# Last attention blocks routed ahead of the early rows' first layer, and the early rows' second layer moved behind the barrier

## The chip, the cores and the metric

The kernel runs on one core of one Trainium2 chip. The metric is device time in microseconds (us) of one execution. Each number of the profile comes from one profiled execution of the kernel, in microseconds from the start of its span.

## The reference, cut to what matters

Chunked attention feeds a mixture of experts in which each token goes to one of eight experts.

```python
batch, n_heads, seq, head_dim = (4, 8, 768, 64); n_mem = 8
chunk, left_ctx, right_ctx = (32, 16, 8)
for c in range(seq // chunk):              # every chunk of 32 queries sees its neighbours and the memory
    scores = scale * q_c @ k_full.T
    out[:, :, c_start:c_end] = softmax(scores) @ v_full
x = out.transpose(0, 2, 1, 3).reshape(3072, 512)
logits = x @ w_gate                        # [3072, 8]
expert_idx = argmax(logits); gate_w = softmax(logits)[expert_idx]
for e in range(8):                         # rows of expert e, w1 [512, 1024], w2 [1024, 512], all float32
    y[rows of e] = relu(x[rows of e] @ w1[e]) @ w2[e]
return gate_w[:, None] * y
```

## The kernel before, in words

The 3,072 tokens are 32 blocks of 96. The loop in `ordinary` (`for i in range(NB)`) makes block i's scores, the values of block i-1 (`values`), and turns block i-2 for its logits (`turn_xb`). Blocks are routed in eight groups, the last two of which are blocks 26 to 28 and 29 to 31. Routing a group (`routed`) is a list of small steps: the best expert of each token, a one-hot matrix, two small matmuls that count how many earlier tokens went to the same expert (`rank`), then `own`, `row` and `where`, which give each token its row in `x_dram`. Only then a block may be scattered there: one indirect DMA on GpSimd per block (`scatter_one`, L848), made to wait for the TensorE instruction that was written down last before it (`behind`).

When 22 blocks are scattered, the first 256 rows of expert 0 are read back (`early_load`, `early_gather`). These are the early rows. Their expert is computed in `early_ops`: a transpose on VectorE (`turn_early`), eight pieces `first(f)` of the first layer (four matmuls of 256 columns each, then a relu on ScalarE, L1093), and before the barrier 384 of the 512 columns of the second layer for their first 128 rows (`part_of`, tile `py0`).

After the loop the code is written out by hand: it sets the order on every engine, since nothing reorders it. It interleaves the last values, the last three blocks' logits (`last_logits`, tile `lg`), the two last groups' routing, the early pieces, the six last scatters, and `count_up`. That counts the tokens of each expert (L973), works out the arm of code for each (`cases`), the first rows (`bases`, L999 to L1001), a check that all softmax sums are sound (`check_sums`, L901 to L903, then a matmul with `okn` and `most`, L1009, which gives `good`), and the row numbers (`rows`, L1025). The second weight matrix of expert 1 (2 MB, L1045) is loaded into the buffer in which the turned blocks (`xTs`) lay, so it waits for the last logits. `end_rows(0)` writes zeros behind expert 0's rows (L965) and needs `bases`.

Then comes a barrier: the sync engine (SP) waits for every DMA and engine (L1846), and every engine waits for the others, before the experts begin. Behind the barrier, `interlude(0)` loads expert 0's other rows (L1420, tile `xs`), opens `sum_r` with two small matmuls, and runs what is left of the early rows' second layer on TensorE (`sum_z`): the last 128 columns for the first 128 rows, then 512 columns for the second 128 rows. After it the first product of expert 0 (`sum_p`) starts. A matmul of float32 is two instructions here: a `first(f)` is eight in the trace, a second layer of 128 rows sixteen.

Of the kernel before, what the change touches and what calls it, by code (L numbers as in the profile page):

```python
# [22 lines left out]
QB = 96  # L23
# [48 lines left out]
NER = 256  # L72
# [10 lines left out]
PAGE = 256  # L83
EARLY_COLUMNS = 384
LB = 16
# [442 lines left out]
def ordinary(ctx, tc, q, k, v, mem_k, mem_v, moe_w_gate, moe_w1, moe_w2, out, good):  # L528
# [180 lines left out]
    def values(i, g, bank):  # L709
        s = st[i]  # L710
        if g == 0:
            s["x"] = xr[:, i % NXR, LB:DX]
        o = bank[0:QB, 0 : 4 * (D + 1)].rearrange("p (h d) -> p h d", h=4)
        for j in range(4):
            h = 4 * g + j
            mm(o[:, j], lhsT=s["ex"][:, h], rhs=s["v"][:, h, 0 : D + 1], start=True, stop=True)

        inv = inv_all[:, i, 4 * g : 4 * g + 4]
        nc.vector.reciprocal(inv, o[:, :, D])
        x = s["x"].rearrange("p (h d) -> p h d", h=H)  # L720
        nc.vector.tensor_tensor(x[:, 4 * g : 4 * g + 4], o[:, :, 0:D], bc(inv, 2, D), op=OP.mult)
    def turn_xb(i):
# [244 lines left out]

    def count_up():

        cnt = cur["bank"][:, 4 * (D + 1) + 8 * E : 4 * (D + 1) + 9 * E + 1]  # L970
        mm(cnt[:, 0:E], lhsT=ones[0:QB], rhs=seen[:, NB], start=True, stop=True)
        mm(cnt[:, E : E + 1], lhsT=ones[0:QB], rhs=okn, start=True, stop=True)
        nc.vector.tensor_tensor(count, cnt[:, 0:E], ebase, op=OP.subtract)  # L973
        nc.vector.tensor_tensor(count[:, 0:1], count[:, 0:1], n0, op=OP.subtract)
# [33 lines left out]
        nc.vector.tensor_scalar(most[:, 0:1], most[:, 0:1], float(XC), None, op0=OP.is_le)  # L1008
        nc.vector.tensor_scalar(most[:, 1:2], cnt[:, E : E + 1], float(QB * 2 * NB * H), None, op0=OP.is_equal)  # L1009
        nc.vector.tensor_tensor(most[:, 0:1], most[:, 0:1], most[:, 2:3], op=OP.mult)  # L1010
# [40 lines left out]

    early_ops = []

# [3 lines left out]

    def second_layer(py, g, fs, sl=slice(0, DM)):
        made = []
        for f in fs:  # L1060
            made.append(
                mm(
                    py,
                    lhsT=h0[:, f, 128 * g : 128 * g + 128],
                    rhs=ms[0]["w2"][:, f, sl],
                    start=f == 0,
                    stop=f == F // 128 - 1,
                )
            )
        return made[0], made[-1]  # L1070

    def early_out(g, py, sl=slice(0, DM)):
        return nc.scalar.activation(early["y", g][:, sl], py, AF.Copy, scale=lab0[:, g, 1:2])

    def early_rows():
# [6 lines left out]

        def first(f):
            ph = ps_s.tile([128, 2, 512], F32, tag="s", name="ph0")[:, 0, 0:NER]
            for c in range(DM // 128):
                mm(
                    ph,
                    lhsT=ms[0]["w1"][:, c, 128 * f : 128 * f + 128],
                    rhs=x0T[:, c],
                    start=c == 0,  # L1090
                    stop=c == DM // 128 - 1,
                )
            nc.scalar.activation(h0[:, f], ph, AF.Relu)  # L1093

        hold = {}

        def part_of(fs, sl):
            if fs[0] == 0:
                hold["y"] = ps_s.tile([128, 2, 512], F32, tag="s", name="py0")
            py = hold["y"][:, 0, 0 : sl.stop - sl.start]  # L1100
            second_layer(py, 0, fs, sl)
            if fs[-1] == F // 128 - 1:
                early_out(0, py, sl)

        early_ops.append(turn_early)
        for f in range(F // 128):
            early_ops.append(lambda f=f: first(f))
# [8 lines left out]
    with tc.manual_schedule():  # L1116
# [19 lines left out]
        for i in range(NB):  # L1136
# [11 lines left out]
            if i <= 23:  # L1148
                routing(1, "p")
            if i >= 1:  # L1150
                values(i - 1, 0, banks[0])
            need(i - 2, turn_xb)
# [3 lines left out]
            if i >= 1:  # L1156
                values(i - 1, 1, banks[1])
            if late:
                place_logits(*late)
            if i > 23:  # L1160
                routing(1, "p")
# [24 lines left out]

        do_early(1)
        n = NB

        def bank_pair():  # L1190
            banks = [ps_o.tile([128, 512], F32, tag="o", name="o") for _ in range(2)]
            cur["bank"] = banks[0]
            return banks
# [11 lines left out]
        routing(99, "v")  # L1205
# [5 lines left out]
        nc.vector.tensor_copy(*late)  # L1211
        do_early(1)
# [6 lines left out]
        banks = bank_pair()  # L1219
        late = last_logits(n - 1, banks[1])  # L1220
        nc.vector.tensor_copy(*late)
        fetch_piece(1)
        work.extend(routed(len(GROUPS) - 1))
        routing(99)
        check_sums()
        do_early(2)
        scatter_some(1)
        routing(1, "p")
        routing(99, "v")
        hold_back()  # L1230
        do_early(1)
        scatter_some(1)
        count_up()
# [5 lines left out]
        while spread:  # L1239
            scatter_some(1)  # L1240
            if len(early_ops) == 2:
                load_index(0)
            do_early(1)
        zeroed = end_rows(0)
# [403 lines left out]
    def interlude(e):  # L1648

        before = ("before", e)  # L1650
        if e == 0:
# [8 lines left out]
            for i in range(3):  # L1660
                sums1[0][0][i]()
            rest_of = slice(EARLY_COLUMNS, DM)
            last = Z[:, 1, 0 : DM - EARLY_COLUMNS]
            op("PE", lambda n: second_layer(last, 0, range(F // 128), rest_of), [], ["z1"], where=before)
            op("ACT", one_op(lambda: early_out(0, last, rest_of)), [], ["z1", "y00"])
            for part in range(4):
# [264 lines left out]
```

## Time and profile before

| | us |
|---|---|
| median of 3 runs (lowest, highest) | 489.65 (489.1, 490.19) |
| the profiled execution | 489.89 |
| its span, first to last instruction | 488.1 |
| attention, routing and early rows | 0 to 164 |
| barrier: TensorE from its last to its next matmul | 164 to 167.3 |
| rest of the early rows' second layer | 167.3 to 179 |
| eight experts | 179 to 480 |

The page counts how long each engine was busy. In 40 slices it also shows the clock that TensorE was granted. A row of the timeline has the start, the time, the engine (PE is TensorE's matmuls, PEld its weight loads, DVE VectorE, ACT ScalarE, POOL GpSimd, SP the sync engine; a q marks an instruction of the engine's queue), the line, the operation, what it writes and reads, and in brackets how long the engine was idle before it and what ended that.

### The profile page before, as it was taken

What the parts mean: (1) busy time and instruction counts of PE and PEld (TensorE: products, weight loads), DVE (VectorE), ACT (ScalarE), POOL (GpSimd) and SP (SyncE); (2) the same over time, 40 slices, a digit from 0 to 9 for tenths busy, and PEclk for the clock granted to TensorE, in tenths of its full rate; (3) what the DMA queues carried; (4) which work ended last, traced back from release to release, by engine and by line L of the source; (5) the groups of instructions that cost most, each with busy time, mean ns of one, the idle gap of its engine ahead of it and who ended that gap; (6) DMA issues with size and microseconds to landing.
All of it is one profiled execution on the core that took longest, in us unless ns stands there. A gap on an engine that the chain in (4) does not pass through costs nothing. (4 is left out here: it accounts for less than half of the span.)

```text
span 488.1 us, 9350 instructions
## 1 busy us (share of the span) xinstructions
PE 464.7 (95%) x3272; PEld 433.3 (89%) x3272; DVE 282.1 (58%) x548; ACT 207.6 (43%) x389; POOL 145.8 (30%) x191
## 2 busy tenths in 40 slices
PE   5899999999999799999999999999999999999992
PEld 4899999999988669999899999977778999989992
DVE  4466677676555556934566667644447776455511
ACT  3676666665622127331452263234313643144312
POOL 2010223323453206623344054113220451253004
PEclk9999999999999889999999999999999999999998
DMA  9999999999886485637696087265510981900002
GB/s 195 179 216 235 219 250 247 232 242 304 225 252 221 122 264 133 198 100 231 182 298 184 3 236 236 60 154 191 145 31 5 299 248 57 281 7 27 1 1 88
DMA packets 104595, 82.99 MB, mean 170 GB/s; under 512 B 41845, under 2 KB 87502, under 8 KB 104528
## 3 DMA queue, kind: packets, MB, share of 16 engines
q1 hardware_dynamic: 96112, 67.95, 54.6%
q0 software_dynamic: 6912, 13.54, 8.5%
q8 instruction: 44, 0.72, 0.6%
q10 hardware_dynamic: 1504, 0.59, 0.5%
q14 instruction: 23, 0.19, 0.1%
HBM read 65.62 MB, written 21.28 MB: 178 GB/s over the span
## 5 line engine op out<-in xcount | busy, mean ns | idle before, releaser
L1455 POOL DMA_INDIRECT out_dram<-y,lab x42 | 49.3, 1175 | 138.7 <-ACT y L1442 30.8
L935 POOL DMA_INDIRECT lab<-x_dram,rows x42 | 52.0, 1238 | 50.8 <-PE sum_q L534 20.8
L534 PE MATMUL o<-v,ex 128*96 128x65 f32 x512 | 52.9, 246 | 0.3 <-issue 0.3
L534 PEld LDWEIGHTS o<-v,ex 128*96 128x96 f32 x512 | 50.5, 165 | 1.8 <-issue 1.6
L534 PE MATMUL sum_p<-xsT,w 128*128 128x144 f32 (+7 forms) x256 | 49.2, 338 | 2.3 <-issue 1.5
L534 PE MATMUL sc<-qT,kT 128*128 128x192 f32 x256 | 49.1, 336 | 0.0
L534 PEld LDWEIGHTS sum_p<-xsT,w 128*128 128x128 f32 x256 | 41.7, 190 | 6.8 <-issue 3.6
L534 PE MATMUL sum_p<-h,w 128*128 128x144 f32 (+7 forms) x256 | 46.1, 335 | 0.0
L848 POOL DMA_INDIRECT x_dram<-xr,dest x32 | 29.7, 927 | 52.8 <-PE o L534 36.3
L705 ACT ACTIVATE ex<-sc,cst 128x256 f32<-128x256 f32 x96 | 38.6, 472 | 14.6 <-PE sc L534 14.2
L534 PEld LDWEIGHTS sum_p<-h,w 128*128 128x128 f32 x256 | 41.8, 190 | 2.4
L1391 ACT COPY sum_r<-sum_p 128x640 f32<-128x640 f32 x36 | 24.4, 678 | 41.5 <-PE sum_p L534 38.7
L534 PEld LDWEIGHTS sc<-qT,kT 128*128 128x128 f32 x256 | 42.0, 195 | 0.0
L656 ACT COPY qT<-tqk 64x384 f32<-64x384 f32 x60 | 30.0, 500 | 28.2 <-PE tqk L539 24.3
L674 DVE COPY kT<-tqk 64x384 f32<-64x384 f32 x60 | 33.1, 552 | 10.5 <-PE tqk L539 9.9
L534 PE MATMUL sum_r<-t,w 128*128 128x144 f32 (+5 forms) x192 | 37.0, 340 | 0.0
L534 PE MATMUL sum_p<-t,s 128*128 128x144 f32 (+5 forms) x192 | 36.9, 340 | 0.0
L534 PE MATMUL sum_q<-t,s 128*128 128x144 f32 (+5 forms) x192 | 36.7, 339 | 0.0
L534 PEld LDWEIGHTS sum_p<-t,s 128*128 128x128 f32 x192 | 31.8, 190 | 2.5
L534 PEld LDWEIGHTS sum_q<-t,s 128*128 128x128 f32 x192 | 31.9, 190 | 2.3
L534 PEld LDWEIGHTS sum_r<-t,w 128*128 128x128 f32 x192 | 31.8, 190 | 2.3
L1409 DVE STREAM_TRANSPOSE xsT<-xs 128x1280 f32<-128x1280 f32 (+1 forms) x16 | 22.4, 1427 | 19.8 <-DMA xs<-x_dram 19.8
(182 smaller groups left out, 774.3 us busy)
## 6 DMA issues: line engine op xcount, KB each, us to landing
w<-in_moe_w_dram SPq DMA_DIRECT2D x128, 128.0 KB
w<-in_moe_w_dram SPq DMA_DIRECT2D x7, 2048.0 KB, 11.4
xs<-x_dram SPq DMA_DIRECT2D x56, 160.0 KB
kn<-in_k_dram SPq DMA_DIRECT2D x16, 384.0 KB
qn<-in_q_dram SPq DMA_DIRECT2D x16, 384.0 KB
x_dram<-zeros SPq DMA_DIRECT2D x8, 396.0 KB, 3.9
v<-in_v_dram SPq DMA_DIRECT2D x24, 128.0 KB
v<-in_v_dram SPq DMA_DIRECT2D x24, 112.0 KB
```

Of the source, the lines that this page charges most:

```text
L534: i = nc.tensor.matmul(*args, **more)
L656: copy(to[:, :, :, t], tq[D * t : D * t + D])
L674: i = copy(to, of[:, :, 0:PAIRS].rearrange("d a (y z p) -> d a y z p", y=2, z=2))
L705: nc.scalar.activation(ex4[:, :, :, sl], sc4[:, :, :, sl], AF.Exp, bias=mask[:, 3 * x + g : 3 * x + g + 1], scale=D**-0.5)
L848: i = nc.gpsimd.indirect_dma_start(out=x_dram, out_offset=bass.IndirectOffsetOnAxis(ap=dest[:, t : t + 1], axis=0), in_=xr[:, t % NXR].bit ...
L935: return nc.gpsimd.indirect_dma_start(out=to.bitcast(I32), out_offset=None, in_=x_dram.rearrange("r (k c) -> (r k) c", c=LB), in_offset=ba ...
L1391: op("ACT", one_op(lambda: nc.scalar.copy(to, of)), reads, writes)
L1409: op("DVE", one_op(lambda: nc.vector.transpose(to, of)), [("xs", y, a) for a in range(4)], [("x", k, 1 - y) for k in range(2)])
L1455: return nc.gpsimd.indirect_dma_start(out=out, out_offset=bass.IndirectOffsetOnAxis(ap=which.bitcast(I32), axis=0), in_=y, in_offset=None, ...
```

## The change

The order behind the loop is written anew. Blocks 29 to 31 get their logits and the two last groups their ranks as early as their inputs allow, in banks of the accumulator memory that the early pieces leave free (`sides`, two tiles of two banks each: the pieces use the first bank, logits and ranks the second). Each first-layer piece is cut into two halves of two matmuls, with routing and scatters between them. The early rows' transpose moves into the loop's last turn. `count_up` becomes a generator that is advanced in three steps; the check of the sums runs behind `bases` instead of ahead of the ranks, and its matmul stands ahead of piece 6. All of the early rows' second layer stands behind the barrier, 512 columns at a time.

```diff
-    def count_up():
-        cnt = cur["bank"][:, 4 * (D + 1) + 8 * E : 4 * (D + 1) + 9 * E + 1]
-        mm(cnt[:, 0:E], lhsT=ones[0:QB], rhs=seen[:, NB], start=True, stop=True)
-        mm(cnt[:, E : E + 1], lhsT=ones[0:QB], rhs=okn, start=True, stop=True)
-        nc.vector.tensor_tensor(count, cnt[:, 0:E], ebase, op=OP.subtract)
+    def count_up(bank, other):
+        cnt = bank[:, 4 * (D + 1) + 8 * E : 4 * (D + 1) + 9 * E]
+        mm(cnt, lhsT=ones[0:QB], rhs=seen[:, NB], start=True, stop=True)
+        yield
+        nc.vector.tensor_tensor(count, cnt, ebase, op=OP.subtract)
...
+        check_sums()
+        yield
+        sound = other[:, 4 * (D + 1) + 9 * E : 4 * (D + 1) + 9 * E + 1]
+        mm(sound, lhsT=ones[0:QB], rhs=okn, start=True, stop=True)
...
-        def first(f):
-            ph = ps_s.tile([128, 2, 512], F32, tag="s", name="ph0")[:, 0, 0:NER]
-            for c in range(DM // 128):
+        def first(f, part):
+            ph, half = sides[f % 2][:, 0, 0:NER], DM // 256
+            for c in range(half * part, half * part + half):
...
-        early_ops.append(lambda: part_of(range(F // 256), slice(0, DM // 2)))
-        early_ops.append(lambda: part_of(range(F // 256, F // 128), slice(0, DM // 2)))
-        early_ops.append(lambda: part_of(range(F // 128), slice(DM // 2, EARLY_COLUMNS)))
...
+            if i == NB - 1:
+                do_early(1)
...
+        sides.extend(ps_s.tile([128, 2, 512], F32, tag="s", name="ph0") for _ in range(2))
         banks = bank_pair()
-        values(n - 1, 0, banks[0])
+        norms = [values(n - 1, 0, banks[0])]
         scatter_some(1)
-        turn_xb(n - 2)
-        late = last_logits(n - 3, banks[1])
-        values(n - 1, 1, banks[1])
+        lg29 = last_logits(n - 3, sides[1][:, 1])
+        norms.append(values(n - 1, 1, banks[1]))
         scatter_some(1)
...
+        turn_xb(n - 2)
+        do_early(1)
+        nc.vector.tensor_copy(*lg29)
+        turn_xb(n - 1)
+        lg30 = last_logits(n - 2, sides[0][:, 1])
+        routing(6, "v")
+        nc.vector.tensor_copy(*lg30)
+        routing(99, "v")
         do_early(1)
         banks = bank_pair()
-        late = last_logits(n - 2, banks[1])
-        nc.vector.tensor_copy(*late)
-        do_early(1)
-        turn_xb(n - 1)
+        lg31 = last_logits(n - 1, banks[1])
+        nc.vector.tensor_copy(*lg31)
...
+        routing(99, "v")
+        do_early(2)
         scatter_some(1)
         do_early(1)
+        scatter_some(1)
+        cur["bank"] = sides[1][:, 1]
         routing(1, "p")
+        counting = count_up(banks[0], sides[0][:, 1])
+        next(counting)
         routing(99, "v")
...
-            op("PE", lambda n: second_layer(last, 0, range(F // 128), rest_of), [], ["z1"], where=before)
+            op("PE", lambda n: second_layer(Z[:, 1], 0, range(F // 128)), [], ["z1"], where=before)
```

What stands on TensorE from the second early piece to the matmul that counts the tokens, before. `ph` are the early pieces, `o<-wg,w` a block's logits, the pairs of 96x24 a group's rank, `seen,ones 128x8` the count and `okn,ones` the check:

```order
L534 MATMUL ph_2155<-x0T,w_1648 128x256 x4
L539 MATMUL tx<-cst,xr 128x96 x4
L534 MATMUL ph_2167<-x0T,w_1648 128x256 x4
L534 MATMUL o<-onehot,cst 96x24
L534 MATMUL o<-seen,ones 96x24
L534 MATMUL o<-wg,w_131 96x8 x4
L534 MATMUL ph_2212<-x0T,w_1648 128x256 x4
L534 MATMUL ph_2218<-x0T,w_1648 128x256 x4
...
L534 MATMUL ph_2234<-x0T,w_1648 128x256 x4
L534 MATMUL o<-seen,ones 128x8
L534 MATMUL o<-okn,ones 128x1
```

Now, in the same place, from the first piece on (`ph_2072` and `ph_2073` are the two side tiles):

```order
L533 MATMUL ph_2072<-x0T,w_1648 128x256 x2
L538 MATMUL tx<-cst,xr 128x96 x4
L533 MATMUL ph_2072<-wg,w_131 96x8 x4
L533 MATMUL ph_2072<-x0T,w_1648 128x256 x2
L533 MATMUL o<-wg,w_131 96x8 x4
L533 MATMUL o<-onehot,cst 96x24
L533 MATMUL o<-seen,ones 96x24
L533 MATMUL ph_2073<-x0T,w_1648 128x256 x4
L533 MATMUL ph_2072<-x0T,w_1648 128x256 x2
L533 MATMUL ph_2073<-onehot,cst 96x24
L533 MATMUL ph_2073<-seen,ones 96x24
L533 MATMUL o<-seen,ones 128x8
```

The last logits stand behind one piece instead of three, and the last rank and the count behind two and a half instead of five and six.

The end of TensorE's list ahead of the barrier (`UNCONDITIONAL_BRANCH`) and the start behind it, before (`py` is the early rows' second layer):

```order
L534 MATMUL ph_2311<-x0T,w_1648 128x256 x4
L534 MATMUL py_2320<-w_1649,h_143 128x256 x4
...
L534 MATMUL py_2320<-w_1649,h_143 128x256 x4
...
L534 MATMUL py_2375<-w_1649,h_143 128x128 x8
L1926 UNCONDITIONAL_BRANCH
L534 MATMUL sum_r<-nought 128x320 x2
L534 MATMUL sum_z<-w_1649,h_143 128x128 x8
L534 MATMUL sum_z<-w_1649,h_143 128x512 x2
```

Now:

```order
L533 MATMUL ph_2072<-okn,ones 128x1
L533 MATMUL ph_2072<-x0T,w_1648 128x256 x4
...
L533 MATMUL ph_2073<-x0T,w_1648 128x256 x2
...
L533 MATMUL ph_2073<-x0T,w_1648 128x256 x2
L1937 UNCONDITIONAL_BRANCH
L533 MATMUL sum_r<-nought 128x320 x2
L533 MATMUL sum_z<-w_1649,h_143 128x512 x10
```

The barrier follows the last early piece at once, and the check's matmul shares a tile with piece 6 right behind it.

VectorE between the first rows and the check, now (before, `ok` and `okn` stood ahead of the last group's ranks, and `most<-o` read a bank that no early piece uses):

```order
L1002 CAST bases<-first_row 128x8
L1003 TENSOR_TENSOR bases<-first_row,held 128x8
L1004 SCALAR_TENSOR_TENSOR bases<-second,first_row 128x8
L904 TENSOR_SCALAR ok<-inv_all 96x256
L905 TENSOR_SCALAR ok<-inv_all 96x256
L906 TENSOR_REDUCE okn<-ok 96x1
L1011 TENSOR_SCALAR most<-count 128x1
L1012 TENSOR_TENSOR most<-count,n_134 128x1
L1013 TENSOR_REDUCE most<-count 128x1
L1014 TENSOR_TENSOR most<-most 128x1
L1015 TENSOR_SCALAR most<-most 128x1
L1016 TENSOR_SCALAR most<-ph_2072 128x1
```

The read of the check's sum (`most<-ph_2072`) comes nine instructions behind `bases`, and piece 6 on TensorE writes the same tile after it.

## Rows read from the trace of the kernel before

**Rows 1.** The page: the span, and busy time of each engine with its share and its number of instructions.

```profile
span 488.1 us, 9350 instructions
...
PE 464.7 (95%) x3272; PEld 433.3 (89%) x3272; DVE 282.1 (58%) x548; ACT 207.6 (43%) x389; POOL 145.8 (30%) x191
```

**Rows 2.** Busy time by stretch: the stretch in us, its length, busy time of PE, PEld, DVE, ACT and POOL with their instructions, the granted clock as a share of the full one, the DMA engines' busy share and GB/s.

```profile
13.50:15.00 1.50, 0.00 (x0) 0.00 (x0) 0.00 (x0) 1.49 (x5) 0.00 (x0) 1.00 1.26 180
15.00:18.00 3.00, 2.92 (x27) 2.95 (x28) 1.16 (x3) 1.98 (x5) 0.00 (x0) 1.00 1.16 178
...
163.00:166.00 3.00, 0.91 (x9) 0.72 (x7) 0.00 (x0) 0.37 (x1) 0.00 (x0) 1.00 0.21 62
166.00:169.00 3.00, 1.67 (x8) 1.56 (x9) 1.71 (x2) 0.00 (x0) 0.99 (x2) 0.59 0.06 11
169.00:172.00 3.00, 3.00 (x13) 2.58 (x13) 1.97 (x2) 1.69 (x3) 0.00 (x0) 0.50 1.03 245
172.00:175.00 3.00, 3.00 (x7) 1.38 (x6) 1.51 (x2) 0.00 (x0) 0.00 (x0) 0.78 0.99 311
175.00:178.00 3.00, 3.00 (x9) 1.33 (x8) 2.93 (x5) 0.00 (x0) 0.00 (x0) 1.00 0.94 291
...
238.00:420.00 182.00, 181.43 (x1044) 167.78 (x1044) 110.50 (x107) 70.22 (x103) 56.09 (x48) 1.00 0.56 159
```

**Rows 3.** Who waited for whom around the barrier (engine and line, what it waited for, us in total, times, longest), and the instructions of the barrier's line on SP (shortest, middle and longest in ns, start of the first and the last).

```profile
SPq L1846 <- DMA x_dram<-xr,dest: 3.6, 1, 3.6
...
PE sum_r L534 <- issue: 3.4, 1, 3.4
...
L1846 SPq EVENT_SEMAPHORE  x12: 4/28/3542, 162.1 to 480.6; - x12
```

**Rows 4.** The timeline ahead of the barrier: TensorE's last early pieces and second layer, and ScalarE's relu and output.

```profile
154.57 3.33 PEld L534 LDWEIGHTS ph<-x0T,w 128*128 128x128 f32 x16
157.92 3.43 PEld L534 LDWEIGHTS py<-w,h 128*128 128x128 f32 x16
158.34 0.38 ACT L1093 ACTIVATE h<-ph 128x256 f32<-128x256 f32 x1 [1.34 <-PE ph L534]
161.86 1.86 PEld L534 LDWEIGHTS py<-w,h 128*128 128x128 f32 x16 [0.51 <-issue]
163.95 0.37 ACT L1073 ACTIVATE y<-py,lab 128x128 f32<-128x128 f32 x1 [1.64 <-PE py L534]
```

**Rows 5.** The timeline behind the barrier.

```profile
167.33 0.71 PE L534 MATMUL sum_r<-nought 128*128 128x320 bf16 x2 [3.41 <-issue]
167.57 4.02 PEld L534 LDWEIGHTS sum_z<-w,h 128*128 128x128 f32 x18
167.83 11.49 PE L534 MATMUL sum_z<-w,h 128*128 128x128 f32 x32
173.49 1.84 DVE L1409 STREAM_TRANSPOSE xsT<-xs 128x768 f32<-128x768 f32 x2 [2.48 <-DMA xs<-x_dram]
178.30 0.19 PEld L534 LDWEIGHTS sum_z<-w,h 128*128 128x128 f32 x1 [0.24 <-issue]
178.73 0.19 PEld L534 LDWEIGHTS sum_p<-xsT,w 128*128 128x128 f32 x1 [0.24 <-issue]
179.16 1.14 PE L534 MATMUL sum_p<-xsT,w 128*128 128x144 f32 x8
```

**Rows 6.** The timeline of the routing chain: the last logits, the weights' load behind them, the check, the last rank, the count and what follows it on VectorE.

```profile
147.92 0.82 PE L534 MATMUL o<-wg,w 128*96 128x8 f32 x8
148.81 0.39 SPq L1045 DMA_DIRECT2D w<-in_moe_w_dram  x1
150.70 0.28 DVE L901 TENSOR_SCALAR ok<-inv_all 96x256 f32<-96x256 f32 x1
151.22 0.68 DVE L903 TENSOR_REDUCE okn<-ok 96x1 f32<-96x512 f32 x1
154.24 0.29 PE L534 MATMUL o<-seen,ones 96*128 96x8 f32 x2
154.78 0.17 DVE L973 TENSOR_TENSOR count<-o,cst 128x8 f32<-128x8 f32 x1 [1.57 <-PE o L534]
158.85 0.15 DVE L1001 SCALAR_TENSOR_TENSOR bases<-second,first_row 128x8 int32<-128x8 f32 x1
159.51 0.15 DVE L1009 TENSOR_SCALAR most<-o 128x1 f32<-128x1 f32 x1
160.47 0.36 SPq L965 DMA_DIRECT2D x_dram<-zeros  x1
162.34 0.18 DVE L1025 TENSOR_SCALAR rows<-far 128x40 int32<-128x40 f32 x1
```

**Rows 7.** Transfers: the last scatter; from a stage of the experts a 2 MB load of weights, the last of a few stores by GpSimd behind it and what waited for their landing; and the page's line on the 2 MB loads (number, size, median us to landing).

```profile
160.68 0.92 POOL L848 DMA_INDIRECT x_dram<-xr,dest  x1 [1.17 <-DVE there L1017]
...
219.04 0.46 SPq L1492 DMA_DIRECT2D w<-in_moe_w_dram  x1
221.75 0.98 POOL L1455 DMA_INDIRECT out_dram<-y,lab  x1 [0.45 <-issue]
228.50 0.11 POOL L1466 MEMSET lab<- 128x5 int32 x1 [5.77 <-DMA out_dram<-y,lab]
...
w<-in_moe_w_dram SPq DMA_DIRECT2D x7, 2048.0 KB, 11.4
```

More of the change, by code (lines that the diff above doesn't have):

```diff
@@ L716, in values, with norm @@
             mm(o[:, j], lhsT=s["ex"][:, h], rhs=s["v"][:, h, 0 : D + 1], start=True, stop=True)
[L718 to L721, printed above, removed]
+        def norm():
+            inv = inv_all[:, i, 4 * g : 4 * g + 4]
+            nc.vector.reciprocal(inv, o[:, :, D])
+            x = s["x"].rearrange("p (h d) -> p h d", h=H)
+            nc.vector.tensor_tensor(x[:, 4 * g : 4 * g + 4], o[:, :, 0:D], bc(inv, 2, D), op=OP.mult)
+        return norm
     def turn_xb(i):
@@ L1008, in count_up @@
         nc.vector.tensor_scalar(most[:, 0:1], most[:, 0:1], float(XC), None, op0=OP.is_le)
-        nc.vector.tensor_scalar(most[:, 1:2], cnt[:, E : E + 1], float(QB * 2 * NB * H), None, op0=OP.is_equal)
+        nc.vector.tensor_scalar(most[:, 1:2], sound, float(QB * 2 * NB * H), None, op0=OP.is_equal)
         nc.vector.tensor_tensor(most[:, 0:1], most[:, 0:1], most[:, 2:3], op=OP.mult)
@@ L1050, in fetch_piece @@
             n -= 1
-    early_ops = []
+    early_ops, sides = [], []
     h0 = epool.tile([128, F // 128, NER], F32, name="h0")
@@ L1070, in second_layer, with early_out @@
         return made[0], made[-1]
-    def early_out(g, py, sl=slice(0, DM)):
-        return nc.scalar.activation(early["y", g][:, sl], py, AF.Copy, scale=lab0[:, g, 1:2])
+    def early_out(g, py):
+        return nc.scalar.activation(early["y", g], py, AF.Copy, scale=lab0[:, g, 1:2])
     def early_rows():
@@ L1092, in first @@
                 )
[L1093 to L1103, printed above, removed]
+            if part == 1:
+                nc.scalar.activation(h0[:, f], ph, AF.Relu)
         early_ops.append(turn_early)
         for f in range(F // 128):
-            early_ops.append(lambda f=f: first(f))
-        early_ops.append(lambda: part_of(range(F // 256), slice(0, DM // 2)))
-        early_ops.append(lambda: part_of(range(F // 256, F // 128), slice(0, DM // 2)))
-        early_ops.append(lambda: part_of(range(F // 128), slice(DM // 2, EARLY_COLUMNS)))
+            for part in range(2):
+                early_ops.append(lambda f=f, part=part: first(f, part))
     def do_early(n):
@@ L1156, in ordinary @@
             if i >= 1:
-                values(i - 1, 1, banks[1])
+                norm = values(i - 1, 1, banks[1])
+                if i < NB - 1:
+                    norm()
             if late:
                 place_logits(*late)
+            if i == NB - 1:
+                norm()
             if i > 23:
@@ L1185, in ordinary @@
                 early_gather()
-        do_early(1)
         n = NB
         def bank_pair():
-            banks = [ps_o.tile([128, 512], F32, tag="o", name="o") for _ in range(2)]
-            cur["bank"] = banks[0]
-            return banks
+            return [ps_o.tile([128, 512], F32, tag="o", name="o") for _ in range(2)]
+        sides.extend(ps_s.tile([128, 2, 512], F32, tag="s", name="ph0") for _ in range(2))
         banks = bank_pair()
-        values(n - 1, 0, banks[0])
+        norms = [values(n - 1, 0, banks[0])]
@@ L1199, in ordinary @@
         scatter_some(1)
-        turn_xb(n - 2)
-        late = last_logits(n - 3, banks[1])
-        values(n - 1, 1, banks[1])
+        lg29 = last_logits(n - 3, sides[1][:, 1])
+        norms.append(values(n - 1, 1, banks[1]))
         scatter_some(1)
-        nc.vector.tensor_copy(*late)
-        routing(99, "v")
+        for norm in norms:
+            norm()
         fetch_w(1, 1)
         fetch_piece(4)
+        turn_xb(n - 2)
+        do_early(1)
+        nc.vector.tensor_copy(*lg29)
+        turn_xb(n - 1)
@@ L1208, in ordinary @@
+        lg30 = last_logits(n - 2, sides[0][:, 1])
+        routing(6, "v")
+        nc.vector.tensor_copy(*lg30)
+        routing(99, "v")
         do_early(1)
         banks = bank_pair()
-        late = last_logits(n - 2, banks[1])
-        nc.vector.tensor_copy(*late)
-        do_early(1)
-        turn_xb(n - 1)
+        lg31 = last_logits(n - 1, banks[1])
+        nc.vector.tensor_copy(*lg31)
+        before_last = list(work)
+        work.clear()
+        work.extend(routed(len(GROUPS) - 1))
@@ L1214, in ordinary @@
+        cur["bank"] = banks[0]
+        before_last.pop(0)[1]()
+        routing(6, "v")
+        for _ in range(3):
+            before_last.pop(0)[1]()
+        spread.extend(f for _, f in before_last)
+        routing(99, "v")
+        do_early(2)
         scatter_some(1)
         do_early(1)
+        scatter_some(1)
+        cur["bank"] = sides[1][:, 1]
         routing(1, "p")
+        counting = count_up(banks[0], sides[0][:, 1])
+        next(counting)
         routing(99, "v")
         hold_back()
-        banks = bank_pair()
@@ L1220, in ordinary @@
-        late = last_logits(n - 1, banks[1])
-        nc.vector.tensor_copy(*late)
         fetch_piece(1)
[L1223 to L1226, printed above, removed]
+        next(counting)
         scatter_some(1)
-        routing(1, "p")
-        routing(99, "v")
-        hold_back()
+        for _ in range(3):
+            do_early(2)
+            scatter_some(1)
         do_early(1)
-        scatter_some(1)
-        count_up()
         index = []
@@ L1237, in load_index @@
             index.append(nc.tensor.value_load(cases[0:1, e : e + 1], min_val=0, max_val=len(arms_of(e)) - 1))
[L1239 to L1243, printed above, removed]
+        for _ in counting:
+            pass
+        do_early(2)
+        load_index(0)
+        do_early(len(early_ops) - 1)
+        assert not spread, len(spread)
         zeroed = end_rows(0)
@@ L1661, in interlude @@
                 sums1[0][0][i]()
-            rest_of = slice(EARLY_COLUMNS, DM)
-            last = Z[:, 1, 0 : DM - EARLY_COLUMNS]
-            op("PE", lambda n: second_layer(last, 0, range(F // 128), rest_of), [], ["z1"], where=before)
-            op("ACT", one_op(lambda: early_out(0, last, rest_of)), [], ["z1", "y00"])
+            op("PE", lambda n: second_layer(Z[:, 1], 0, range(F // 128)), [], ["z1"], where=before)
+            op("ACT", one_op(lambda: early_out(0, Z[:, 1])), [], ["z1", "y00"])
             for part in range(4):
```

7 lines of the change are left out of this document (3 added, 4 removed).

## The prediction

> **What bounds the kernel now.** I read the page first. TensorE is busy 464.7 of 488.1 us [rows 1], and from 238 to 420 us it lacks 0.6 of 182 us [rows 2]: the experts are one TensorE queue, and what starts them earlier ends the kernel earlier by as much. So I looked at the one place inside where the table of stretches shows it idle and slow, the barrier between 164 and 167.3. The list of waits names both sides: TensorE waits 3.4 us for its next matmul, and SP stands 3.54 us, from 162.1 on, for the landing of a scatter into `x_dram` [rows 3]. That ends near 165.7, while TensorE's last output was taken from 163.95 on [rows 4]. So the last scatter releases the barrier, some 1.7 us behind TensorE, and from there to TensorE's first matmul at 167.33 [rows 5] are 1.6 us of engines meeting.
>
> The second loss is the clock. [...] What that costs follows from the same instructions at both levels: 16 weight loads with 128 columns take 1.86 us at full clock [rows 4]; with 512 columns one follows another in 0.43 [rows 5]. Sixteen of each would be 1.86 + 16 x 0.43 = 8.7 us, but from 167.57 to 178.73 they took 11.16: 2.4 us lost. With some 0.25 of the two opening matmuls that is 2.65.
>
> Expert 0's own rows don't bound the start: their transposes run from 173.49 for 1.84 us, done at 175.3, while `sum_p` starts at 179.16 [rows 5].
>
> **The change part by part.** *Logits and count earlier.* The last logits started at 147.92 behind three early pieces. Sixteen weight loads of pieces begin at 154.57 and the next work at 157.92 [rows 4], so a piece is 1.7, and 1.75 with the step to other work. Now two pieces and a rank (0.3) fewer stand ahead: 147.9 - 3.5 - 0.3 = 144.1, plus one new wait. The second half of piece 0 stands behind VectorE's copy of block 30's logits, taken from the same side tile; that copy waits for the logits just ahead of it, 0.4 by the reach of a matmul's result. So 144.5. The 2 MB load of weights, which followed those logits at 148.81 [rows 6], starts at 145.4. Behind the logits (0.7) come a rank (0.3), a piece and a half (2.65), the last rank (0.3): the count starts at 148.4 instead of 154.24 [rows 6], 5.8 us earlier. VectorE's chain to `bases` took from 154.78 to 159.0, now 149.0 to 153.2.
>
> *The check late.* It takes 1.2 us (150.70 to 151.90 [rows 6]), now 153.2 to 154.4. Ahead of the routing chain it hid in VectorE's wait for the rank; now it stands on the way to `good` and `rows`. TensorE has half a piece and three pieces behind the count (148.6 + 0.9 + 5.25 = 154.75), so the check's matmul waits for nothing. But piece 6 waits until VectorE has read that sum: 0.6 us of small steps, the read (0.15) and the step to TensorE: 155.3. TensorE loses 0.4. `rows` came 3.0 us behind that read (159.51 to 162.52 [rows 6]): 158.3, ahead of TensorE's end.
>
> *Second layer away from the front.* Pieces 6 and 7 follow at 155.3 and end at 158.8. I add 0.3, since TensorE lost 0.51 at the loads and the branch that stand there [rows 4] and these now fall between the halves of piece 7: 159.1, where the old order came to 163.95. The halves cost nothing themselves: same matmuls, and another bank's work between them. The relu (0.38 and 0.04 to start) ends at 159.55 and is the last engine's work.
>
> *The scatters.* Each waits for the matmul written ahead of it. The last stands behind the first half of piece 5: 153.9, on GpSimd at 154.0 instead of 160.68 [rows 7]. No row shows how long it lands beside the 2 MB load, so I bound it. It took 5.0 us before (160.68 to 165.7), beside the zeros issued at 160.47 [rows 6]: 159.0. A store behind a 2 MB load had landed at 228.50, 6.75 us after its issue at 221.75, 9.5 after the load's [rows 7]: 160.75. I take the nearer row, a scatter, 159.0, ahead of the relu. The load itself, by the median of 11.4 us [rows 7], lands at 156.8. The zeros, 1.6 us behind `bases` as before, are issued at 154.8.
>
> *Barrier and behind it.* 159.55 + 1.6 = 161.15 for TensorE's restart, a gap of 2.05 us instead of 3.4. Does the clock fall in it? The trace has both: a stretch of 1.5 us without a matmul, 13.5 to 15.0, after which the share stayed 1.00, and 3.4 us after which it was 0.59 [rows 2, 3]. I take the nearer row, no fall. Then 0.25 for the opening and 32 x 0.43 = 13.76 for two second layers at 512 columns, with 0.15 to fill: `sum_p` at 175.3. The transposes, 8.0 us behind the restart as before, are done at 169.2 and stay hidden, now by 6 us.
>
> [...]
>
> *Sum.* The restart comes 167.33 - 161.15 = 6.2 us earlier. From restart to `sum_p` it was 11.83 us and becomes 14.15, 2.3 more (16 x (0.43 - 0.116) = 5.0 of added columns, less 2.65 of slow clock). The gain is 179.16 - 175.3 = 3.85 us, of a span of 488.1 and a time of 489.89, which has 1.8 around it and lies 0.24 above the median. 489.65 - 3.85 = 485.8.
>
> **The rivals.** *The transfers set the barrier, the clock holds.* At the upper bound, landing at 160.75, the restart is 162.35 and `sum_p` 176.5: gain 2.65, **487.0**. For it: SP waited on just such a landing before, and six scatters, the zeros and the load now overlap. Against it: the last scatter goes out 6.7 us earlier, TensorE is done only 4.85 earlier.
>
> [...]
>
> *The clock falls all the same.* The slow stretch took (0.41 + 0.50 + 0.22) x 3 = 3.4 us of clock [rows 2], some 0.4 of it before the restart: 3.0 for work that starts with it. Gain 0.85, **488.8 to 488.9**. For it: the gap of 2.05 lies between the two that the trace shows. Against it: it is nearer to the harmless one.
>
> *Slower: the scatters land only behind the whole load, and the clock falls in the long gap.* The load is done at 156.8 (median row), then 6 x 203 KB (96 rows of 528 words) and 396 KB of zeros at 311 GB/s, the most that the transfers behind the barrier reached [rows 2], are 5.2: landing at 162.0, restart 163.6, and 14.15 + 3.0 behind it: `sum_p` at 180.75, **491.2**. With the fallen clock it decides from a landing at 160.4 on (160.4 + 1.6 + 17.15 = 179.15). Against it: SP saw the last scatter land within 5.0.
>
> *Nothing arrives.* The experts would wait for weights or rows by what they start earlier: **489.6**. Against it: TensorE lacks 0.6 of 182 us behind the start, and loads wait for TensorE's progress, so they move with it.
>
> **How the numbers follow.** Forecast 0.62 (its own range 485.1 to 486.6, from a wait of 0 to 0.4 at the copy and 0 to 1 at the check and the branch), transfers 0.13, clock 0.13, slower 0.06, nothing 0.06. A difference of 0.2%, 1.0 us, is about what a measurement of this kernel can tell from none: faster means below 488.7. The forecast, the transfers and some 0.05 of the clock case lie there: 0.80. The rest of that case and the last give 0.14, the slower case 0.06. For 8 in 10 the range goes from 485.0, without new waits, to 488.9, the clock case: 485.0 to 488.9.
>
> **What would show it.** Right: `sum_r` starts near 161.2 behind some 2 us of idle TensorE, the share stays 1.00 there, SP's last wait at the barrier is for ScalarE, `sum_z` is 32 instructions of 0.43, `sum_p` starts near 175.3, the 2 MB load is issued near 145.4, the count near 148.4. Wrong: SP waits at the barrier for a scatter or the load; a share of 0.5 behind it; TensorE stands longer than 0.5 us ahead of piece 6; or the last product of expert 7 does not end 3.8 us earlier although `sum_p` started so.

## The result, and the profile after

The changed kernel takes 492.96 us (median of 20 runs), the kernel before 487.67 beside it (also 20): the ratio is 1.0079, 95% interval 1.0056 to 1.0101. It is slower by 0.8%, where the forecast said 485.8. The ratios here leave out runs that lie over 1.5% above the fastest of their kernel, five of the 20 here; the medians do not. The three runs that the forecast started from had a median of 489.65, so the kernel before is itself some 2 us faster than it looked.

The profiled execution took 495.07 us, 2.1 more than the median of its kernel; its span is 493.3, 5.2 more than the span of before. First the timeline of TensorE in the changed kernel, from the check's matmul to the first product of expert 0 (start, length, engine, line and operation, what ended the idle time ahead):

```profile
157.45 0.28 PE L533 MATMUL ph<-okn,ones 96*128 96x1 f32 x2
157.98 2.86 PE L533 MATMUL ph<-x0T,w 128*128 128x256 f32 x12 [0.25 <-DVE most L1016]
164.34 1.13 PE L533 MATMUL ph<-x0T,w 128*128 128x256 f32 x4 [3.50 <-issue]
167.08 0.71 PE L533 MATMUL sum_r<-nought 128*128 128x320 bf16 x2 [1.61 <-issue]
167.59 16.45 PE L533 MATMUL sum_z<-w,h 128*128 128x512 f32 x32
183.87 1.14 PE L533 MATMUL sum_p<-xsT,w 128*128 128x144 f32 x8
```

Piece 6 and half of piece 7 run behind `most`, as forecast, but 2.7 us late. Then TensorE stands for 3.50 us between the two halves of piece 7, with "issue" as the reason: no engine and no transfer that the profile links to it. The restart at 167.08 is where it was before (167.33 [rows 5]), and `sum_p` starts 4.7 us later than before. What stands between the halves is the load of the flag, the hint and the jump that `addr_align` makes. That line alone, in the changed kernel (times in ns: shortest, middle, longest; then its start):

```profile
L1263 PEldq COMPARE_BRANCH  x1: 3683/3683/3683, 160.6 to 160.6; - x1
```

The same jump in the kernel before:

```profile
L1250 PEldq COMPARE_BRANCH  x1: 365/365/365, 161.4 to 161.4; - x1
```

And what the DMA engines of the changed kernel did from 161 to 164.2, in 40 slices of 0.08 us (busy tenths, then GB/s) and by queue:

```profile
DMA  1000009000000000000000000000000000000000
GB/s 53 0 0 0 0 0 205 0 0 0 0 0 0 0 0 0 0 0 0 0 0 0 0 0 0 0 0 0 0 0 0 0 0 0 0 0 0 0 0 0
...
q8 instruction: 1, 0.02, 2.5%
```

One packet of 16 KB (205 GB/s for 0.08 us) on the queue for instructions starts near 161.5, 0.9 us behind the jump's start; the jump ends some 2.7 us after that, at 164.28.

The stretches show two more things: TensorE stands at 138 to 141, and its granted clock is 0.81 from 141 to 150 and 0.76 from 167 to 179 (stretch, length, busy time of PE, PEld, DVE, ACT, POOL, clock, DMA share, GB/s). The changed kernel:

```profile
138.00:141.00 3.00, 2.02 (x27) 1.87 (x22) 2.53 (x7) 0.01 (x1) 1.91 (x2) 1.00 0.95 211
141.00:150.00 9.00, 8.75 (x58) 7.85 (x58) 4.47 (x27) 1.68 (x5) 2.95 (x9) 0.81 0.75 234
...
167.10:179.00 11.90, 11.90 (x23) 5.25 (x24) 9.70 (x10) 2.01 (x3) 0.99 (x2) 0.76 0.86 245
```

Before, in the same stretches:

```profile
138.00:141.00 3.00, 2.71 (x30) 2.43 (x29) 1.98 (x5) 0.96 (x2) 1.54 (x3) 1.00 0.89 263
141.00:150.00 9.00, 9.00 (x61) 8.12 (x61) 4.22 (x26) 1.91 (x6) 2.03 (x6) 1.00 0.44 146
```

VectorE's timeline names the wait at 138 in the changed kernel, and TensorE's next matmul follows it:

```profile
137.95 1.25 DVE L1086 STREAM_TRANSPOSE x0T<-x 128x1024 f32<-128x1024 f32 x1 [1.96 <-DMA x<-x_dram]
139.12 0.14 DVE L719 RECIPROCAL inv_all<-o 96x4 f32<-96x4 f32 x1
139.29 0.42 DVE L721 TENSOR_TENSOR xr<-o,inv_all 96x256 f32<-96x256 f32 x1
...
139.92 0.86 PE L533 MATMUL o<-v,ex 128*96 128x65 f32 x8 [0.98 <-DMA w<-in_moe_w_dram]
```

The change put `turn_early` ahead of block 30's norms. On VectorE the norms now stand behind a transpose that waits 1.96 us for the load of the early rows; the first of them starts at 139.12, as the transpose ends. TensorE, whose next values need the bank that the norms read, stands 0.98 us until 139.92; the last logits start at 147.18, not at 144.5. The profile puts this wait down to a load of weights, and in two of the runs below to something else; but in all five profiles with this order TensorE goes on 0.21 us behind the end of the norms' second instruction (here 139.71).

### The profile page after: what moved, and what is told of

Same layout as the page of the kernel before. It is cut to its first block, busy times and chain, and to the rows that moved or that the text cites. A ratio compares the mean times of both kernels' runs of the same rounds, so it can differ in the third digit from the quotient of the medians.

```text
span 493.3 us, 9287 instructions
## 1 busy us (share of the span) xinstructions
PE 466.7 (95%) x3240; PEld 431.1 (87%) x3240; DVE 281.9 (57%) x548; ACT 207.1 (42%) x387; POOL 146.4 (30%) x191
```

## Experiments: the jump

Theory F: the 3.50 us are the fetch of the program block that the jump leads to, asked for too late. `addr_align(PAGE, 0, 0)`, with the kernel's `PAGE` of 256, jumps to the next multiple of 256 instructions; a block is here what lies between two of them, and that it is fetched as a whole is part of the theory. The change took some 40 instructions from ahead of the jump (16 matmul instructions of the second layer, four of piece 7, and their weight loads), so the jump stands elsewhere in its block than before. One added jump at TensorE's first instruction shifts all of its program and nothing else (the first run, e1). Its second number, the slot, says where in a block the program goes on:

```diff
     with tc.manual_schedule():
+        nc.tensor.addr_align(PAGE, 131, 0)
         load_k(0)
```

> The changed kernel with one alignment jump added at TensorE's first instruction, where TensorE stands idle for 5.8 us in any case; it shifts the whole TensorE program so that the jump ahead of the second half of piece 7 comes about 100 instructions after a multiple of 256, by a count of the records. Nothing else changes. Theory F (the 3.50 us are the fetch of the program block that the jump leads to, asked for too late): the COMPARE_BRANCH at L1263 goes from 3.68 to about 0.4 us, the gap of 3.50 ahead of the last four ph matmuls to below 0.6, TensorE restarts behind the barrier 3 to 4 us sooner (163 to 164), the time falls by 3 to 6 us to 487 to 490, more where the clock now holds. Rival W (the jump waits for the loads of the flag and the arm number, or for the hint just ahead of it): the gap stays at 3.5 and the time within 0.5 us of the changed kernel's.

Measured: 489.95 us against 488.41, ratio 1.0022 (0.9986 to 1.0057). The jump takes 0.33 us, the gap is 0.50, and the clock behind the barrier holds. The timeline:

```profile
158.08 2.95 PE L533 MATMUL ph<-x0T,w 128*128 128x256 f32 x12 [0.25 <-DVE most L1016]
161.54 1.13 PE L533 MATMUL ph<-x0T,w 128*128 128x256 f32 x4 [0.50 <-issue]
164.32 0.45 PE L533 MATMUL sum_r<-nought 128*128 128x320 bf16 x2 [1.66 <-issue]
164.61 13.90 PE L533 MATMUL sum_z<-w,h 128*128 128x512 f32 x32
178.34 1.14 PE L533 MATMUL sum_p<-xsT,w 128*128 128x144 f32 x8
```

No wait, load or matmul was taken away, so rival W falls.

The same with slot 20 in place of 131 (the second run, e3), so that by a count of the records the jump stands about 12 instructions ahead of a multiple of 256. That the fetch was asked for earlier there was my assumption; at which instruction it is asked for is not shown:

> [...] Theory F: no stall here either, branch about 0.4 us, time as in the run before within 1 us. Rival W: gap 3.5 us, time as the changed kernel's. A third reading, that any shift of the program costs or gains by where later jumps fall, would show in the windows behind 240 us and not here.

Measured: 488.27, ratio 0.9993 (0.9962 to 1.0023); jump 0.33 us, restart 165.00, `sum_p` 179.02. Again no stall. Its third reading, a later jump, falls as well: from the start of `sum_p` to the end of the span it takes 308.9 to 310.4 us in all fourteen profiles of this document, so the time is decided ahead of `sum_p`.

The kernel before with slot 5, to bring the stall there (the third run, e2):

> The kernel before with the same added jump, its TensorE program shifted so that the jump ahead of the second half of the second layer comes about 13 instructions after a multiple of 256, as in the changed kernel. Theory F: the stall appears in the kernel before: COMPARE_BRANCH from 0.37 to 2 to 4 us, the gap ahead of the last py matmuls from 0.51 to 2 to 4, the restart behind the barrier later by 2 to 3 us, the time by 2 to 5 us to 490 to 493. Rival W: no change, 487.7 within 0.5 us.

Measured: 491.57 against 488.41, ratio 1.0076 (1.0038 to 1.0113). The kernel before has the stall too, at the same place, when its program is shifted. First the jump's line, then TensorE's timeline:

```profile
L1251 PEldq COMPARE_BRANCH  x1: 3356/3356/3356, 160.4 to 160.4; - x1
```

The timeline has the gap of 3.14 us ahead of the last `py` matmuls, and the restart:

```profile
163.83 3.57 PE L534 MATMUL py<-w,h 128*128 128x128 f32 x16 [3.14 <-issue]
169.09 0.45 PE L534 MATMUL sum_r<-nought 128*128 128x320 bf16 x2 [1.69 <-issue]
169.37 8.82 PE L534 MATMUL sum_z<-w,h 128*128 128x128 f32 x32
178.02 1.14 PE L534 MATMUL sum_p<-xsT,w 128*128 128x144 f32 x8
```

Its last line carries a second finding: at full clock `sum_p` follows the restart by 8.93 us, not by the 11.83 of the profile that the forecast used.

Two slots between, in the changed kernel (82, e11, and 62, e12):

> The changed kernel with the added jump of the first run, shifted so that the jump ahead of the second half of piece 7 comes about 50 instructions after a multiple of 256, some 4 us behind it in time. Theory F1 (the next block is asked for when TensorE's sequencer enters a block, and takes some 3.3 us, as long as the branches of 3.35 to 3.68 us in the stalled runs): no stall, branch 0.3 to 0.5 us. Rival F2 (it is asked for only well inside a block, or by the jump itself): branch 3.3 to 3.7 us.

> The same at about 30 instructions after the multiple of 256, which TensorE's sequencer passes some 2.5 us ahead of the jump, behind its wait for the count of the checks. F1: part of a stall, branch 0.5 to 1.5 us. F2: 3.3 to 3.7 us.

One run each: 495.92 and 493.53 us, the kernel before 487.4 beside them. The jumps, first of slot 82, then of slot 62:

```profile
L1264 PEldq COMPARE_BRANCH  x1: 3102/3102/3102, 160.9 to 160.9; - x1
```

```profile
L1264 PEldq COMPARE_BRANCH  x1: 1925/1925/1925, 161.6 to 161.6; - x1
```

These two don't decide between F1 and F2: F1 had no stall for slot 82, F2 a full one for slot 62, and neither came. The offsets in the expectations were counted from the trace, which lacks some records, so "50" and "30" may be off by tens, and the later offset stalled more. The transfers tell more. In slot 82, from 161 to 164.2 in slices of 0.08 us, the 16 KB are the only packet, near 161.68:

```profile
GB/s 0 0 0 0 0 0 0 0 205 0 0 0 0 0 0 0 0 0 0 0 0 0 0 0 0 0 0 0 0 0 0 0 0 0 0 0 0 0 0 0
```

The jump ends 2.4 us later. In slot 62, from 160.4 on in slices of 0.08 us, it is the 205 GB/s near 161.15, behind the last scatters:

```profile
GB/s 370 370 238 502 185 343 106 0 106 205 53 0 0 0 0 0 0 0 0 0 0 0 0 0 0 0 0 0 0 0 0 0 0 0 0 0 0 0 0 0
```

That is 0.45 us ahead of the jump, and the jump ends 2.4 us after it: the jump takes 1.2 to 1.8 us less than the four whose packet starts 0.8 to 1.0 us behind theirs. This fits a jump that waits for its block: in all five stalled profiles (these three, e2 and e5 below) it ends 2.4 to 2.7 us behind the start of such a packet, and in the nine others the last one ahead of the jump came 4.7 to 18 us before it (in the kernel before at 156.72, its jump starts at 161.4). Behind the end of the jump the next packet starts within 0.7 to 1.3 us in all fourteen (0.75 in the changed kernel, 1.29 in the kernel before), which fits F1, a jump into a block followed by the fetch of the next. Why the fetch came so late ahead of the five jumps, and at which instruction it is asked for when no jump leads into the block, stays open.

## Experiments: the early transpose

The first run's kernel with `turn_early` back behind the loop, as before (the fourth run, e4):

```diff
-            if i == NB - 1:
-                do_early(1)
...
-                norm = values(i - 1, 1, banks[1])
-                if i < NB - 1:
-                    norm()
+                values(i - 1, 1, banks[1])()
...
+        do_early(1)
         n = NB
```

> The first run's kernel (the jump in the middle of a block, so no stall at it), and in addition the transposition of the early rows x0T put back behind the loop, as in the kernel before, so that block 30's norms no longer wait behind it for the x0 load. Theory X (x0T waits for the load and holds block 30's norms, TensorE stands for about 0.9 us at 139 to 140 and the clock falls at 142 for 3.4 us because of it): no idle time of TensorE of over 0.4 us at 138 to 141, granted clock 1.00 instead of 0.81 in 141 to 150, last logits at 144.5 to 145.5 instead of 147.28, restart behind the barrier at 161.5 to 162.5 instead of 164.32, sum_p at 175.5 to 176.5, the time 2 to 3 us under the first run's 489.95, 486.5 to 488. Rival N (the earlier stages only shift, the scatters or the barrier's other waits land no sooner): the restart stays at 164 and the time within 0.7 us of the first run's. A third reading (the clock falls at 142 for another cause, such as the pieces between the logits): no idle time, but 0.81 stays and half of the gain is missing.

Measured: 487.76 us, ratio 1.0009 (0.9983 to 1.0035). In its profile (486.29 us) the timeline of TensorE is:

```profile
157.96 1.13 PE L533 MATMUL ph<-x0T,w 128*128 128x256 f32 x4 [0.48 <-issue]
161.12 0.45 PE L533 MATMUL sum_r<-nought 128*128 128x320 bf16 x2 [2.04 <-issue]
161.40 13.90 PE L533 MATMUL sum_z<-w,h 128*128 128x512 f32 x32
175.14 1.14 PE L533 MATMUL sum_p<-xsT,w 128*128 128x144 f32 x8
```

and the two stretches at the norms:

```profile
138.00:141.00 3.00, 3.00 (x33) 2.92 (x32) 2.85 (x9) 0.48 (x1) 1.33 (x2) 1.00 0.82 214
141.00:150.00 9.00, 8.55 (x58) 7.58 (x57) 5.74 (x39) 1.97 (x6) 6.18 (x14) 1.00 0.88 298
```

TensorE no longer stands, the clock holds, the last logits start at 143.44 and the restart comes 3.2 us sooner: theory X, in the trace. Of these 3.2 us, 1.1 were there at the last scores already (135.00 in e1, 133.86 here), ahead of the transpose. From there to the last logits it takes 12.2 to 13.5 us in the five profiles with the transpose ahead of the norms and 9.6 in the five with it put back. All five profiles with the transpose ahead of the norms have VectorE waiting 1.7 to 3.3 us for that load and a share of 0.81 from 141 to 150; the nine without it have neither. In the times the step is smaller, 489.95 to 487.76, with intervals of the ratios that overlap: that it shortens the run is not shown.

The changed kernel with that edit alone, the stall left in (e5):

> The changed kernel with x0T put back alone, the program not shifted. If the two losses add, the jump's stall is still there (branch 3 to 3.7 us) and the time is 2 to 3 us under the changed kernel's 492.96: 490 to 491. If the stall grows by what comes earlier ahead of it (the fetch ends at a fixed time), it stays at about 492.5.

Measured: 492.74, ratio 1.0087 (1.0052 to 1.0121). The jump takes 3.32 us, and nothing is gained over the changed kernel, although in the one profile `sum_p` starts at 179.67, 4.2 earlier than there. That the two losses add is not borne out. The two profiles are not of like executions: the granted clock, averaged over the run, is 0.980 in the changed kernel's and 0.988 here, while the middle run of either kernel has 0.986. Why the runs gain nothing stays open. From the stalled to the unstalled one it is 5.0 us (492.74 to 487.76; the ratios' intervals lie apart).

The fourth run's kernel with all of piece 7 ahead of the jump (e6):

```diff
-        do_early(len(early_ops) - 1)
+        do_early(len(early_ops))
...
         nc.tensor.addr_align(PAGE, 0, 0)
-        do_early(1)
```

> The kernel of e4 with the second half of piece 7 issued ahead of the jump instead of behind it, so that nothing but the barrier stands behind the jump. If the 0.5 us of loads and jump lie beside the relu and its wait, the restart comes 0.3 to 0.6 us sooner than in e4 and the time falls by as much; if the barrier's own steps (some 13 waits of 0.1 us and a branch) follow the jump in any case, no change within 0.3 us.

Measured: 487.10, ratio 0.9975 (0.9939 to 1.0011), restart at 160.27. Inconclusive: its last scatter also landed 0.8 us sooner than in e4.

## Experiments: the second layer

A control of the shift, the kernel before with slot 100 (e10):

> The kernel before with the same added jump at TensorE's first instruction, shifted so that the jump ahead of the last part of the second layer comes about 108 instructions after a multiple of 256, as in the first run: a control of the shift, and a second profile of the kernel before. Expected: the time of the kernel before within 0.2%, 487.5 to 489; branch about 0.4 us. Theory B (the profile of before that the forecast went from held a fall of the clock behind the barrier that the kernel does not always have): where the clock holds at 1.00 from 167 to 179, sum_p follows the restart by 8.9 us as in the third run (176 to 176.5 at a restart of 167.3), not by 11.8. Rival: sum_p waits for the transpositions of xsT, and follows by 11 to 12 us at any clock.

Measured: 488.58 against 487.26, ratio 1.0030 (1.0005 to 1.0056), a little slower, for no reason that the profile shows. If the added jump costs this, the other shifted kernels are as much too slow; that is not shown. Its timeline bears out theory B: here the clock held behind a gap as long as in the profile of before. This profile is the fastest of its 12 runs (486.62 us), and that of before lay 2 us over its median, so neither stands for the middle run.

```profile
166.37 0.45 PE L534 MATMUL sum_r<-nought 128*128 128x320 bf16 x2 [3.42 <-issue]
166.65 8.82 PE L534 MATMUL sum_z<-w,h 128*128 128x128 f32 x32
175.31 1.14 PE L534 MATMUL sum_p<-xsT,w 128*128 128x144 f32 x8
```

At full clock the kernel before starts `sum_p` at 175.31, as early as the forecast's 175.3 for the changed one.

The kernel before with only the second layer moved behind the barrier (`EARLY_COLUMNS = 0`, the three `part_of` pieces taken out, shifted off the stall; e7):

> The kernel before, shifted off the stall, with only one part of the change: all 512 columns of the early rows' second layer stand behind the barrier and none ahead of it; routing, banks and check stay where they were. Theory W (TensorE's work in all stays the same, so the move gains only the idle time that it fills): the pieces end some 5 us sooner, the restart comes at 164 to 165.5 (then held by the row numbers on VectorE, 162.34 in before, and the barrier's steps), sum_p 13.8 to 14 us behind it at full clock, 178 to 179.3, that is 1.5 to 3 us later than the kernel before has it at full clock, and the time 1 to 3 us over before's, 489 to 491. Rival (the forecast's reading): the move costs nothing, since sum_p waited for xsT until 178.73 in any case: the time within 0.5 us of before's.

Measured: 492.33 against 487.26, ratio 1.0105 (1.0075 to 1.0136). The timeline:

```profile
165.97 0.71 PE L534 MATMUL sum_r<-nought 128*128 128x320 bf16 x2 [7.22 <-issue]
166.47 15.88 PE L534 MATMUL sum_z<-w,h 128*128 128x512 f32 x32
182.19 1.14 PE L534 MATMUL sum_p<-xsT,w 128*128 128x144 f32 x8
```

Theory W, and more than its 1 to 3 us: the work of TensorE stays, and the restart gains only 0.4 us on the control (165.97 for 166.37, not the 164 to 165.5 expected). In the kernel before, whose routing it keeps, the barrier waits for the last scatter [rows 3]. And the clock falls in the gap of 7.22 us: its share is 0.60 from 163 to 166, 0.50 to 169 and 0.76 to 172, so the 32 instructions take 15.88 us, not 13.90.

The fourth run's kernel with 384 columns ahead of the barrier again (e8):

```diff
+EARLY_COLUMNS = 384
...
+        early_ops.append(lambda: part_of(range(F // 256), slice(0, DM // 2)))
+        early_ops.append(lambda: part_of(range(F // 256, F // 128), slice(0, DM // 2)))
+        early_ops.append(lambda: part_of(range(F // 128), slice(DM // 2, EARLY_COLUMNS)))
```

> The fourth run's kernel (x0T back, no stall) with the second layer's first 384 columns ahead of the barrier again, as in the kernel before: the rest of the change alone (order of routing, banks, the late check, halved pieces). Theory W: restart later by the 5.3 us of py and less of the 2.04 us gap, at 165 to 166.5, sum_p 8.9 us behind it at full clock, 174 to 175.4, the time within 0.7 us of e4's 487.76. Rival: with the barrier later, more waits end at it, restart over 167 and no gain over before is left, 488.5.

Measured: 486.40 against 487.26, ratio 0.9985 (0.9967 to 1.0004), restart 165.62, `sum_p` 174.55, clock 1.00: theory W, though the time is 1.4 us under e4's, where 0.7 was allowed. The rest of the change alone gains nothing that is clear of noise.

The same with one part of 128 columns (`EARLY_COLUMNS = 128`), in the gap ahead of the restart (e9):

> The fourth run's kernel with 128 of the 512 columns of the second layer (8 matmuls, 1.78 us by the py rows of before) ahead of the barrier, in the time in which TensorE stands between piece 7 and the restart (2.04 us in e4, where the barrier waited for the last scatter). If that gap is free, the restart stays within 0.8 us of e4's 161.12 and sum_p comes 0.9 to 1.7 us sooner than e4's 175.14 at full clock; the time falls by as much, 486 to 487, under both kernels. If the barrier's steps follow TensorE's last matmul, the restart is 1.5 to 2 us later and nothing is gained.

Measured: 485.33 against 487.26, ratio 0.9967 (0.9945 to 0.9988). It beats both kernels. The timeline:

```profile
158.01 1.95 PE L534 MATMUL ph<-w,h 128*128 128x128 f32 x16
161.59 0.45 PE L534 MATMUL sum_r<-nought 128*128 128x320 bf16 x2 [1.64 <-issue]
161.88 12.19 PE L534 MATMUL sum_z<-w,h 128*128 128x384 f32 x32
173.90 1.14 PE L534 MATMUL sum_p<-xsT,w 128*128 128x144 f32 x8
```

The restart moves by 0.47 us against e4 and `sum_p` comes 1.24 sooner.

## Why the prediction was wrong

*Logits and count earlier.* "Plus one new wait" was the first wrong step: the sum had the copy's wait (0.4, my estimate, where a piece's relu starts 0.44 us behind its last weight load, 158.34 for 157.90 [rows 4]; measured 0.25), not the one of block 30's norms behind `x0T`. The logits, the load of weights (148.01) and the count (151.10) are each 2.6 to 2.7 us late, 0.5 of it already at the last scores (134.79 for 134.26 before), the rest by it. Without it (e4) the logits start at 143.44 and the count at 147.74, 0.7 to 1.1 ahead of the forecast.

*The check late.* Right: TensorE waits 0.25 ahead of piece 6, where I had 0.4.

*Second layer away from the front.* "I add 0.3, since TensorE lost 0.51 at the loads and the branch" is the step that made the kernel slower. The price of that row was a price of where the jump stood in its block, and the edit moved it. The jump alone took 0.37 us in the kernel before, 3.68 in the changed kernel, with the start of a 16 KB packet on the instruction queue inside it, and 3.36 in the kernel before with its program shifted (e2). The nine jumps of 0.33 to 0.44 us have the last such packet 4.7 to 18 us ahead of them, the four of 3.1 to 3.7 us have it 0.8 to 1.0 us behind their start, and the one of 1.93 has it 0.45 ahead. The stall removed alone is worth 3.0 us in the medians (492.96 to 489.95; ratio 1.0079 to 1.0022).

*The scatters.* The nearer bound was the better one: in e4 the last one goes out at 153.66 and the sync engine waits for its landing until 159.4, where I had 154.0 and 159.0. It took 5.7 us, not 5.0.

*Barrier and behind it.* In e4 the gap is 2.04 us, the clock holds, the restart is at 161.12 and `sum_p` at 175.14; the forecast had 2.05, 161.15 and 175.3. That the restart agrees is luck. The forecast put it 1.6 us behind the end of the last relu, a figure read off a barrier that waited for a scatter. The sync engine's waits and the relu, first in the changed kernel, then in e4:

```profile
SPq L1857 <- ACT h L1101: 4.1, 1, 4.1
165.51 0.38 ACT L1101 ACTIVATE h<-ph 128x256 f32<-128x256 f32 x1 [5.11 <-PE ph L533]
...
SPq L1853 <- DMA x_dram<-xr,dest: 3.1, 1, 3.1
159.12 0.38 ACT L1101 ACTIVATE h<-ph 128x256 f32<-128x256 f32 x1 [2.09 <-PE ph L533]
```

Where the relu is the last, the restart follows its end by 1.2 us (165.89 to 167.08). In e4 that would make 160.7, by my estimate from these rows; but there the sync engine waits for the scatter, as in the first rival, and the restart is 1.7 us behind the 159.4, as far as in the kernel before (165.6 to 167.33). So a step that I had 0.4 too long and a landing that I had 0.4 too early came to the same time.

In the changed kernel the stall and the barrier put gaps of 3.50 and 1.61 us within 6.3 us, and the clock fell, as in the second rival: its share is 0.50 from 167.1 to 172 and 0.88 from there to 175. From restart to `sum_p` it takes 16.79 us, where e1 and e4 at full clock take 14.02.

*Sum.* Two errors stand here. The chain's size in the profile is explained: `sum_p` at 183.87 is 8.6 us behind the forecast, 2.7 up to piece 6, 3.2 at the jump (3.50 for the 0.3 that I added) and 2.6 behind the restart, from the clock (16.79 for 14.15), nearly all of it. The time misses by less, 7.2 us (492.96 for 485.8), since this execution lies 2.1 us over its median. The other is the base. I counted the 2.65 us of slow clock behind the barrier as a loss that the change removes. The control shows the kernel before in an execution without it, and the median of the kernel before lies 2 us under the profiled execution. How many of its runs have that loss is not shown. So e4 meets the forecast of its time in the profile (486.29 for 485.8) and is still no faster than before in the runs (1.0009): at full clock the order of the change gains 0.2 us on the control's `sum_p` (175.14 against 175.31), since the restart comes 5.25 us sooner and 5.1 of added `sum_z` (13.90 for 8.82) follow it.

*The rivals.* The falling clock came, with a price of 2.8 for the 3.0 I had, but in a gap that I did not foresee. The scatters landed at 159.4 (e4) and not at the 162.0 of the slower case. No rival had the jump, and none had the norms.

## What to carry to other kernels

Where instructions are moved or removed ahead of an aligned jump, its time can change (3.1 to 3.7 us here for 0.4, with the start of a packet on the instruction queue inside it), and the row of the old program does not price it: look for the instruction queue's packet, and shift the program by one jump in an idle place to test it. A step moved ahead in an engine's list brings its own waits with it (1.7 to 3.3 us of VectorE here), and what stood ahead of it before now pays them. A loss seen in one profiled execution, above all one of the clock, is counted as a gain only if more profiles or the median show that most runs have it.

## What was not expected of the hardware

A jump took 0.33 to 0.44 us where the last packet on the instruction queue had come 4.7 us or more ahead of it, 3.1 to 3.7 where it started 0.8 to 1.0 us behind the jump's start, and 1.93 where it started 0.45 us ahead of it.

The length of a gap alone does not say whether the clock falls. Behind 3.41 us it fell in the kernel before (0.59 from 166 to 169 [rows 2, 5]) and behind 3.42 us it held at 1.00 in the control. Behind the idle stretch from 13.5 to 15.0, after which the forecast found it at 1.00 [rows 2], it was 0.62 from 15 to 18 in the changed kernel (TensorE idle for 1.59 us in the kernel before, 1.80 in the changed one), and it fell there in three of the fourteen profiles. Behind 138 to 141 it fell (0.81 from 141 to 150) in all five profiles in which TensorE lost 0.75 to 2.12 us there, four of them less than the 2.04 us at the barrier behind which it held in e4 (2.39 in e6).
